# Eight-group cross network on one core: a joint first pass over two output tiles, tails copied by VectorE, and a rearranged last job

## Chip, cores and metric

The kernel runs on one core of one Trainium2 chip. The metric is the device time of one execution in microseconds (us), the median over several executions. A profile is one execution taken by the hardware profiler. Its span, from the first to the last recorded instruction, is about 1.8 us shorter than the device time of the same execution.

Engines are named as in the profile: PE is the matrix engine, PEld its weight load, ACT the scalar engine, DVE the vector engine, SP the engine that issues most DMAs ("SPq" and "ACTq" are rows of DMA issues).

## The reference

`x0` is [16384, 416], `ws` is [6, 416, 416], `bs` is [6, 416], all bf16.

```python
def reference(x0, ws, bs):
    x = x0
    for l in range(ws.shape[0]):
        proj = jnp.einsum('bd,de->be', x, ws[l]) + bs[l]
        x = x0 * proj + x
    return x
```

## The kernel before

The rows are cut into 8 groups of 2048. A job is one layer of one group. Data lie transposed on the chip, features on partitions: 416 features are three tiles of 128 and a "tail" of 32, and the 2048 rows are four chunks of 512 (`NJ = 4`). For one output tile, PE adds up the products with three input tiles (12 matmuls of 512 columns) and with the tails (4 matmuls on 32 partitions) in four PSUM banks; ACT evicts two banks at a time and adds the bias; DVE multiplies by x0 and adds x. Jobs of different groups alternate so that PE always has work. The program has eight banks and uses four per output tile, so an output tile has to wait for the eviction of the one before the last; where it comes too early the profile lists the wait (`PE ps L460 <- ACT tw L398`, 0.4 us in the changed kernel).

Group 0 starts from row-major loads that PE transposes. Group 1 is brought in by DMA transposes while group 0's first layer runs, and its tails are copied out of a staging tile (`Tb`) by four small DMAs:

```python
def load_group(g):
    ...
    turn(0)
    add("sp", lambda h: h.dma_start_transpose(Tb, x0[rows, D - P:D]), ...)
    turn(1)
    turn(2)
    for j in range(NJ):
        q = slice(j * T32, (j + 1) * T32)
        add("sp", lambda h, q=q, j=j: h.dma_start(x0s[s][q, XW:XW + CH], Tb[P - T32:P, j * CH:(j + 1) * CH]),
            reads=[("ost", 0, 0)], writes=[("x03q", s, j)], lane=f"x03_{s}", batch=g)
    if g == 1:
        load_wm(1, "sp")
        load_w3(1, "sp")
```

The last job (group 7, layer 5) is computed with rows on partitions, so that its result can be stored without a transpose. It goes in four quarters `kk`. For the residual x it needs x turned row-major: tiles 0 and 1 by DMA transposes (`rest_turn`), tile 2 and the tails by PE (`turn_last`, `turn_tails`). The store of group 6, whose result was turned just before, shares the DMA queue with them:

```python
def rest_turn(t):
    ...
    for j0, j1 in ((0, NJ),) if t == 0 else ((0, 2), (2, NJ)):
        if t and j0:
            store(LAST - 1, 0, 1)          # 416 KB of group 6
        add("sp", lambda h, j0=j0, j1=j1: h.dma_start_transpose(
            x5f[:, j0 * KK:j1 * KK, t * P:(t + 1) * P], xs[s][:, t * GC + j0 * CH:t * GC + j1 * CH]), ...)

def turn_tails(bks):                        # 16 small transposes, four banks
    for kk in range(KK):
        for j in range(NJ):
            r, q = quad(g, l, j)
            add("pe", lambda h, ...: h.matmul(
                psum_t(b)[:, kk * T32:(kk + 1) * T32], x3col(j, kk), ident[q, q], is_transpose=True, ...), ...)
    ...                                     # one ACT copy out of the four banks
# last job:
store(LAST - 1, 1, 2)
store(LAST - 1, 2, NJ)
...
for kk in range(1, KK):
    nat_rows(kk, bks[kk])
    for j in range(NJ):
        nat_full(kk, j, bks[kk][j], False)  # matmuls
        nat_out(kk, j, bks[kk])             # ACT
        ...                                 # DVE: nat_mul, nat_add
    if kk < last:
        nat_store(kk, 0, NJ)                # 416 KB each
```

## Time and profile before

| | kernel before |
|---|---|
| device time, median of 3 (lowest to highest) | 477.18 us (476.61 to 477.33) |
| span of the profiled execution | 476.1 us |
| PE, DVE, ACT busy | 98%, 85%, 72% |
| PE's waits at the second group's start | 0.8 us (input tile 2), 0.8 us (tails) |
| DVE's wait in the last job | 1.25 us (residual's second half-transpose) |

The lines behind this stand in the prediction. A row of the timeline reads: start in us, duration, engine and line of the program, operation, what it writes and reads, how many instructions, and in brackets how long the engine stood idle before it and what it then was waiting for. A row of the waits reads: what waited, for what, the sum in us, how often, the longest.

### The profile page before, as it was taken

The numbers are of one execution on the slowest core, as the hardware profiler recorded it, in microseconds if no ns is written. First come the engines' busy times: TensorE is split into PE (matmuls) and PEld (weight loads), VectorE is DVE, ScalarE is ACT, GpSimd is POOL, SyncE is SP. The second block draws the span as 40 slices with busy tenths as digits, with TensorE's granted clock in tenths as the row PEclk, the third lists the DMA queues.
The fourth block names the chain that finished last, engine by engine and source line by source line (L and its number), as shares of the span: only waits on it lengthen the run. The fifth ranks groups of instructions, "written<-read, shape, count | busy, mean of one in ns | idle before, by whom it ended". The sixth has DMA issues, their size and how long they took to land.

```text
span 476.1 us, 8364 instructions
## 1 busy us (share of the span) xinstructions
PE 467.7 (98%) x3356; PEld 193.4 (41%) x3356; DVE 403.3 (85%) x695; ACT 341.7 (72%) x371; POOL 5.8 (1%) x15
## 2 busy tenths in 40 slices
PE   8899999999999999999999999999999999999995
PEld 5344444444444444444444444444444444444342
DVE  2788888888888888898889879888888888888886
ACT  4577777777777777777777777777777777777785
POOL 1000000000000000000000000000000000000000
PEclk9999999999999999999999999999999999999999
DMA  8966860630102397369318941980000039025898
GB/s 223 161 163 150 174 122 1 144 79 0 30 7 43 64 224 154 81 143 246 77 25 195 220 95 26 175 264 0 2 12 23 8 64 240 12 45 122 226 192 247
DMA packets 138859, 53.31 MB, mean 112 GB/s; under 512 B 112442, under 2 KB 138308, under 8 KB 138820
## 3 DMA queue, kind: packets, MB, share of 16 engines
q1 hardware_dynamic: 138664, 52.67, 49.6%
q8 instruction: 26, 0.43, 0.4%
q10 hardware_dynamic: 156, 0.11, 0.1%
q14 instruction: 13, 0.11, 0.1%
HBM read 5.97 MB, written 13.63 MB: 41 GB/s over the span
## 4 chain that ended last, share of the span: by engine, by line
PE 90%; SPq 4%; DVE 3%; DMA 2%; ACT 0%; issue 0%; DVEq 0%
PE ps L457 75%; PE ps L478 7%; PE ps L498 7%; SPq L292 2%; DMA x<-x 1%; PE ps L472 1%; DVE x L887 1%; SPq L522 1%; DVE x L881 1%; DVE x L409 1%; DVE tw L404 1%; PE ps L489 1%; SPq L297 0%; ACT tw L395 0%; DMA x<-ost 0%; SPq L303 0%
## 5 line engine op out<-in xcount | busy, mean ns | idle before, releaser
L395 ACT ACTIVATE tw<-ps,bias 128x1024 bf16<-128x1024 f32 (+1 forms) x295 | 299.6, 1070 | 121.4 <-PE ps L478 82.2
L457 PE MATMUL ps<-x,wm 128*128 128x512 bf16 x1692 | 379.6, 380 | 1.3 <-DMA x<-in_x_dram 0.8
L457 PEld LDWEIGHTS ps<-x,wm 128*128 128x128 bf16 x1692 | 158.7, 98 | 215.3 <-issue 28.2
L404 DVE TENSOR_TENSOR tw<-tw,x 128x1024 bf16<-128x1024 bf16 (+1 forms) x285 | 192.8, 684 | 55.6 <-ACT tw L395 55.2
L409 DVE TENSOR_TENSOR x<-tw,x 128x1024 bf16<-128x1024 bf16 (+1 forms) x285 | 182.5, 681 | 0.0
L478 PE MATMUL ps<-x,w 32*128 32x512 bf16 x512 | 39.2, 379 | 0.8 <-DMA x<-ost 0.8
L498 PE MATMUL ps<-x,wm 128*32 128x512 bf16 x564 | 33.0, 380 | 0.0
L435 ACT ACTIVATE ts<-ps,bias 128x512 bf16<-128x512 f32 x47 | 28.7, 700 | 0.0
L498 PEld LDWEIGHTS ps<-x,wm 128*32 128x32 bf16 x564 | 13.8, 96 | 17.6 <-issue 5.3
L439 DVE TENSOR_TENSOR x<-ts,x 128x512 bf16<-128x512 bf16 x47 | 18.6, 418 | 2.4 <-DMA x<-x 2.4
L478 PEld LDWEIGHTS ps<-x,w 32*128 32x128 bf16 x512 | 7.8, 92 | 28.5 <-issue 27.1
L437 DVE TENSOR_TENSOR ts<-ts,x 128x512 bf16<-128x512 bf16 x47 | 18.6, 418 | 0.0
L821 PE MATMUL ps<-wm,x 128*128 128x416 bf16 x48 | 9.5, 340 | 0.0
L684 POOL COPY ost<-ot 128x512 bf16<-128x512 bf16 x6 | 4.3, 720 | 423.7 <-DMA ot<-x 423.7
L875 ACT ACTIVATE x<-ps 128x416 bf16<-128x416 f32 x16 | 7.7, 534 | 2.0 <-PE ps L821 1.9
L575 DVE COPY x<-ps 128x512 bf16<-128x512 bf16 x5 | 2.0, 422 | 8.2 <-PE ps L565 8.1
L577 ACT ACTIVATE x<-ps 128x512 bf16<-128x512 bf16 x7 | 3.8, 595 | 4.9 <-PE ps L565 4.9
L821 PEld LDWEIGHTS ps<-wm,x 128*128 128x128 bf16 x48 | 4.3, 98 | 4.2 <-issue 1.0
L887 DVE TENSOR_TENSOR x<-x,x 128x832 bf16<-128x832 bf16 (+1 forms) x9 | 4.8, 542 | 1.4 <-DMA x<-x 1.3
L489 PE MATMUL ps<-x,w 32*32 32x512 bf16 x188 | 5.9, 374 | 0.0
L472 PE MATMUL ps<-x,w 32*32 32x512 bf16 x208 | 5.6, 385 | 0.0
L881 DVE TENSOR_TENSOR x<-x,x 128x832 bf16<-128x832 bf16 (+1 forms) x10 | 4.8, 500 | 0.7 <-ACT x L875 0.7
(40 smaller groups left out, 32.0 us busy)
## 6 DMA issues: line engine op xcount, KB each, us to landing
out_dram<-ost SPq DMA_DIRECT2D x6, 1664.0 KB, 7.2
x<-x SPq DMA_DIRECT2D x24, 96.0 KB, 2.1
wm<-in_ws_dram SPq DMA_DIRECT2D x6, 312.0 KB, 3.4
x<-in_x_dram SPq DMA_DIRECT2D x8, 208.0 KB, 4.2
x<-in_x_dram SPq DMA_DIRECT2D x4, 416.0 KB, 8.0
x<-x SPq DMA_DIRECT2D x22, 64.0 KB, 2.0
out_dram<-x SPq DMA_DIRECT2D x3, 416.0 KB, 3.6
x<-ost SPq DMA_DIRECT2D x28, 32.0 KB, 2.0
```

The lines of the kernel that those rows point to most:

```text
L395: add("act", lambda h, a=a, w=w, b0=b0: h.activation(tw[r][:, a * CH:(a + w) * CH], psum[:, b0 * CH:(b0 + w) * CH], ACT_F.Identity, bias=b ...
L404: add("dve", lambda h, a=a, e=e: h.tensor_tensor(tw[r][:, a * CH:e * CH], tw[r][:, a * CH:e * CH], x0s[s0][:, i * GC + a * CH:i * GC + e * ...
L409: add("dve", lambda h, a=a, e=e: h.tensor_tensor(xs[so][:, i * GC + a * CH:i * GC + e * CH], tw[r][:, a * CH:e * CH], src(i, a, e), ALU.ad ...
L435: add("act", lambda h: h.activation(ts[r][:, :], bank(b), ACT_F.Identity, bias=bias[:, 3, l:l + 1], scale=1.0), reads=[("ps", b), "bias"], ...
L437: add("dve", lambda h: h.tensor_tensor(ts[r][:, :], ts[r][:, :], x03, ALU.mult), reads=[("ts", r)] + tok0, writes=[("ts", r)], release=True)
L439: add("dve", lambda h: h.tensor_tensor(x3s[so][:, :], ts[r][:, :], res, ALU.add), reads=[("ts", r)] + rtok, writes=[("x3", so), ("x3", so, ...
L457: add("pe", lambda h, t=t, j=j: h.matmul(bank(banks[j]), wm[l][:, t, ecols], src(t, j, j + 1), start=(first and t == 0), stop=(not first a ...
L472: add("pe", lambda h, q=q, j=j, r=r, c=c, o=o: h.matmul(psum[o, banks[j] * CH:(banks[j] + 1) * CH], w3[l][q, i * P + c * T32:i * P + (c + ...
L478: add("pe", lambda h, q=q, j=j, r=r: h.matmul(bank(banks[j]), w3[l][q, ecols], src[q, :], start=first, stop=not first, tile_position=(r * ...
L489: add("pe", lambda h, l=l, b=b, s3=s3, ri=ri, qi=qi, ro=ro, qo=qo: h.matmul(psum[qo, b * CH:(b + 1) * CH], w3[l][qi, NT * P:D], s3[qi, :], ...
L498: add("pe", lambda h, t=t, j=j, src=src, l=l, b=b, ro=ro, qo=qo: h.matmul(psum[qo, b * CH:(b + 1) * CH], wm[l][:, t, NT * P:D], src(t, j, ...
L821: add("pe", lambda h, t=t: h.matmul(bank(b, n=D), xcol(t, j, kk), wm[l][:, t, :], start=(first and t == 0), stop=(not first and t == NT - 1)),
```

## The change

The intent: at the start, let PE work on input tiles 0 and 1 of group 1 for two output tiles before it needs tile 2 and the tails, and take the tails' DMAs away. At the end, let the second half-transpose go directly behind the first, and use fewer and larger PE transposes for the tails so that fewer banks are held.

```diff
@@ load_group
-        for j in range(NJ):
-            ... h.dma_start(x0s[s][q, XW:XW + CH], Tb[P - T32:P, j * CH:(j + 1) * CH])
-        if g == 1:
-            load_wm(1, "sp")
-            load_w3(1, "sp")
+        if g > 1:
+            for j in range(NJ):
+                ... the same four DMAs
+            rotate_x03(g)
@@ before group 0's last tile
+    def second_tails():
+        for j in range(NJ):
+            add("dve", lambda h, q=q, j=j: h.tensor_copy(
+                x0s[s][q, XW:XW + CH], Tb[P - T32:P, j * CH:(j + 1) * CH]), ...)
+        load_wm(1, "sp") ... load_w3(2, "sp")
@@ rest_turn
-            if t and j0:
-                store(LAST - 1, 0, 1)
@@ the first two output tiles of group 1
+    def two_tiles(g, l):
+        bks = [job_banks(), job_banks()]
+        for t in (0, 1):
+            for i in (0, 1):
+                full(g, l, i, bks[i], True, False, ts_=[t])
+        full(g, l, 0, bks[0], True, False, ts_=[2])
+        rows32(g, l, 0, bks[0], False)
+        evacuate(g, l, 0, bks[0], list(range(NJ)), 2)
+        finish_tile(g, l)
+        rows32(g, l, 1, bks[1], False, inner=True)
+        full(g, l, 1, bks[1], False, False, ts_=[2])
+        evacuate(g, l, 1, bks[1], list(range(NJ)), 2)
+        finish_tile(g, l)
@@ turn_tails: four full transposes in one bank, two ACT copies
-            for j in range(NJ):
-                ... h.matmul(psum_t(b)[:, kk * T32:(kk + 1) * T32], x3col(j, kk), ident[q, q], is_transpose=True)
+            add("pe", lambda h, kk=kk: h.transpose(
+                psum_t(b)[:, kk * P:(kk + 1) * P], s3[:, kk * P:(kk + 1) * P], ident[:, :]), ...)
@@ last job
-    store(LAST - 1, 1, 2)
+    store(LAST - 1, 0, 2)
     store(LAST - 1, 2, NJ)
-    turn_tails([b0, b1, b2, b3])
+    turn_tails(b0)
```

More of the change, by code (lines that the diff above doesn't have):

```diff
@@ L300, in load_group, with rotate_x03 @@
         turn(2)
-        for j in range(NJ):
-            q = slice(j * T32, (j + 1) * T32)
-            add("sp", lambda h, q=q, j=j: h.dma_start(x0s[s][q, XW:XW + CH], Tb[P - T32:P, j * CH:(j + 1) * CH]),
-                reads=[("ost", 0, 0)], writes=[("x03q", s, j)], lane=f"x03_{s}", batch=g)
-        if g == 1:
-            load_wm(1, "sp")
-            load_w3(1, "sp")
+        if g > 1:
+            for j in range(NJ):
+                q = slice(j * T32, (j + 1) * T32)
+                add("sp", lambda h, q=q, j=j: h.dma_start(
+                    x0s[s][q, XW:XW + CH], Tb[P - T32:P, j * CH:(j + 1) * CH]),
+                    reads=[("ost", 0, 0)], writes=[("x03q", s, j)], lane=f"x03_{s}", batch=g)
+            rotate_x03(g)
+    def rotate_x03(g):
+        s = slot(g)
         if turn_of(g, 1):
@@ L448, in prefill, with full @@
             rotate(x3s[xtail[(g, l)]], x3s[so], n, [("x3", xtail[(g, l)])], ("x3", so), f"rot{so}", (g, l))
-    def full(g, l, i, banks, first, chunk_major, after_chunk=None, chunks=range(NJ)):
+    def full(g, l, i, banks, first, chunk_major, after_chunk=None, chunks=range(NJ), ts_=range(NT)):
         src, stok = x_src(g, l)
         ecols = slice(i * P, (i + 1) * P)
-        seq = [(t, j) for j in chunks for t in range(NT)] if chunk_major else \
-              [(t, j) for t in range(NT) for j in chunks]
+        seq = [(t, j) for j in chunks for t in ts_] if chunk_major else \
+              [(t, j) for t in ts_ for j in chunks]
         for t, j in seq:
@@ L462, in full, with rows32 @@
                 after_chunk(j)
-    def rows32(g, l, i, banks, first, small=False):
+    def rows32(g, l, i, banks, first, small=False, inner=False):
         src, stok = x3_src(g, l)
@@ L478, in rows32 @@
             add("pe", lambda h, q=q, j=j, r=r: h.matmul(
-                bank(banks[j]), w3[l][q, ecols], src[q, :], start=first, stop=not first,
+                bank(banks[j]), w3[l][q, ecols], src[q, :], start=first and not inner,
+                stop=not first and not inner,
                 tile_position=(r * T32, 0)),
@@ L536, in bass_standalone__cross_network_dcn__recsys_kernel @@
     load_group(1)
-    load_wm(2, "sp")
-    load_w3(2, "sp")
+    def second_tails():
+        s = slot(1)
+        for j in range(NJ):
+            q = slice(j * T32, (j + 1) * T32)
+            add("dve", lambda h, q=q, j=j: h.tensor_copy(
+                x0s[s][q, XW:XW + CH], Tb[P - T32:P, j * CH:(j + 1) * CH]),
+                reads=[("ost", 0, 0)], writes=[("x03q", s, j)])
+        load_wm(1, "sp")
+        load_w3(1, "sp")
+        rotate_x03(1)
+        load_wm(2, "sp")
+        load_w3(2, "sp")
     def keep_busy(n, b):
@@ L627, in first_job @@
         evacuate(g, l, 1, bb, list(range(NJ)), 2)
+        second_tails()
         full(g, l, 2, ba, False, True, lambda j: evacuate(g, l, 2, ba, [j], 1))
@@ L776, in bass_standalone__cross_network_dcn__recsys_kernel @@
     mode[len(items) - 1] = "RF"
+    def two_tiles(g, l):
+        assert items[:2] == [("tile", (g, l), 0), ("tile", (g, l), 1)]
+        bks = [job_banks(), job_banks()]
[10 more added lines that the diff above has]
+        finish_tile(g, l)
     first_job()
@@ L786, in bass_standalone__cross_network_dcn__recsys_kernel @@
             start_job(g, l)
+        if n == 0:
+            two_tiles(g, l)
+            continue
+        if n == 1:
+            continue
         if mode[n] in ("FR", "F1"):
@@ L844, in turned_out, with turn_tails @@
             add("dve", lambda h: h.tensor_copy(dst, sp_), **kw)
-    def turn_tails(bks):
+    def turn_tails(b):
         for kk in range(KK):
-            for j in range(NJ):
-                r, q = quad(g, l, j)
-                add("pe", lambda h, b=bks[j], j=j, kk=kk, q=q, r=r: h.matmul(
-                    psum_t(b)[:, kk * T32:(kk + 1) * T32], x3col(j, kk), ident[q, q], is_transpose=True,
-                    tile_position=(r * T32, 0)),
-                    reads=tok3 + ["ident"], writes=[("ps", bks[j])])
-        b = bks[0]
-        assert bks == list(range(b, b + NJ))
-        sp_ = psum[:, b * CH:(b + NJ) * CH].bitcast(BF16).rearrange("p (j c) -> p j c", j=NJ)[:, :, 0:KK * T32]
-        add("act", lambda h: h.activation(
-            x5n[:, :, :, NT * P:D], sp_.rearrange("p j (k f) -> p j k f", k=KK), ACT_F.Copy),
-            reads=[("ps", b) for b in bks] + ["x5 free"], writes=[("x5n", j, NT) for j in range(NJ)])
+            add("pe", lambda h, kk=kk: h.transpose(
+                psum_t(b)[:, kk * P:(kk + 1) * P], s3[:, kk * P:(kk + 1) * P], ident[:, :]),
+                reads=tok3 + ["ident"], writes=[("ps", b)])
+        sp_ = psum_t(b)[:, 0:KK * P].rearrange("p (k q f) -> p q k f", k=KK, q=NJ)
+        j = 0
+        while j < NJ:
+            r = quad(g, l, j)[0]
+            n = min(NJ - j, NJ - r)
+            add("act", lambda h, j=j, r=r, n=n: h.activation(
+                x5n[:, j:j + n, :, NT * P:D], sp_[:, r:r + n, :, :], ACT_F.Copy),
+                reads=[("ps", b), "x5 free"], writes=[("x5n", a, NT) for a in range(j, j + n)])
+            j += n
     def nat_rows(kk, bks, first=True):
```

## The prediction

> **What bounds the kernel now.** I read the page's busy shares first, then the waits of TensorE, then the chain that ended last, and then the timeline of the two ends of the kernel.
>
> ```profile
> PE 467.7 (98%) x3356; PEld 193.4 (41%) x3356; DVE 403.3 (85%) x695; ACT 341.7 (72%) x371; POOL 5.8 (1%) x15
> ...
> PE 90%; SPq 4%; DVE 3%; DMA 2%; ACT 0%; issue 0%; DVEq 0%
> ```
>
> TensorE (PE) is busy 98% of a span of 476.1 us, and 90% of the chain is PE. The middle has nothing to give: the diff leaves the number of large matmuls as it is. What can move is the 10% of the chain that is not PE, and PE's own waits:
>
> ```profile
> PE ps L457 <- DMA x<-in_x_dram: 0.8, 1, 0.8
> PE ps L478 <- DMA x<-ost: 0.8, 1, 0.8
> ...
> PE ps L832 <- ACT x L857: 0.4, 1, 0.4
> PE ps L850 <- ACT tw L395: 0.2, 1, 0.2
> ```
>
> The first two are each one wait at the start of the second group; the last two are in the final job. The timeline shows the first pair in place:
>
> ```profile
> 18.36 1.90 PE L457 MATMUL ps<-x,wm 128*128 128x512 bf16 x8
> ...
> 21.08 1.04 PE L457 MATMUL ps<-x,wm 128*128 128x512 bf16 x4 [0.82 <-DMA x<-in_x_dram]
> ...
> 22.89 0.61 PE L478 MATMUL ps<-x,w 32*128 32x512 bf16 x8 [0.77 <-DMA x<-ost]
> 23.32 2.12 ACT L395 ACTIVATE tw<-ps,bias 128x1024 bf16<-128x1024 f32 x2 [3.85 <-PE ps L478]
> 23.43 5.35 PE L457 MATMUL ps<-x,wm 128*128 128x512 bf16 x24
> ```
>
> Eight matmuls of the second group's first output tile use input tiles 0 and 1; then PE waits for input tile 2, which a DMA transpose is still bringing, and then for the tails (the last 32 features), which four small DMAs copy out of the staging tile. Those are issued at 19.04 to 20.96 and the last takes 1.88 us to land. From 23 us on PE waits for nothing until the last job. There the chain leaves PE:
>
> ```profile
> 452.40 0.38 PE ps L478 x4
> 452.79 2.11 ACT tw L395 x2
> ...
> 460.91 5.35 DMA x<-x
> ...
> 466.38 0.59 DVE x L887
> ```
>
> and the timeline of the DMA queue and of VectorE (DVE) shows why:
>
> ```profile
> 458.89 1.34 SPq L705 DMA_TRANSPOSE x<-x  x1
> 460.40 0.45 SPq L691 DMA_DIRECT2D out_dram<-ost  x1
> 460.91 1.44 SPq L705 DMA_TRANSPOSE x<-x  x1
> ```
>
> ```profile
> 464.54 0.59 DVE L887 TENSOR_TENSOR x<-x,x 128x832 bf16<-128x832 bf16 x1
> 466.38 0.59 DVE L887 TENSOR_TENSOR x<-x,x 128x832 bf16<-128x832 bf16 x1 [1.25 <-DMA x<-x]
> ```
>
> The second half-transpose of the last residual is issued behind a quarter store (416 KB), lands 5.35 us after issue, and DVE stands still for 1.25 us. From 466.38 DVE runs without a gap longer than 0.2 us to 473.8, so those 1.25 us reach the end.
>
> [...] the rate rises from about 205 GB/s to 355 at 461.5, when the store runs, and the three residual transposes take 3.2, 4.5 and 5.4 us to land, the longest being the one behind the store. [...] the 32 KB tail copies take 2.0 us (median)[...]. [...] The kernel before has no such copy on DVE; its 128x512 adds come every 0.33 us (two in 0.75), so I take 0.2 to 0.33 us for each 32x512 copy. [...]
>
> **The change, part by part.**
>
> One pass over input tiles. The first two output tiles of group 1 now run as 8 matmuls on input tile 0, 8 on tile 1, 4 on tile 2, 8 tail matmuls, 4 on tile 2. The pitch of a large matmul is 5.29/24 = 0.2204 us. Starting at 18.36, the first 16 end their issue at 18.36 + 3.53 = 21.89, after 21.08 when tile 2 was there: the 0.82 us wait goes. The tail matmuls come at 18.36 + 20 x 0.2204 = 22.77. Their data is now copied by DVE, in its queue behind the adds that end at 18.72: 4 copies, 0.8 to 1.3 us, done by 20.1. The 0.77 us wait goes as well. The 8 tail matmuls take 0.54 (the chain's step), the last 4 take 0.88: all of it is issued by 24.19. Before, the same work (12 of the 24 matmuls from 23.43) was issued by 23.43 + 12 x 0.2204 = 26.08. That is 1.89 us earlier: 1.59 of waits, and about 0.3 of drain around them.
>
> What is given back. The next job takes the banks of the first output tile. ScalarE (ACT) starts evicting them about 0.45 us after the tail matmuls start (22.89 to 23.32 before): at about 23.25. It needs 2.12 us for the two pairs of banks, so they come free at about 24.35 and 25.4. Before, PE had 12 matmuls between; now it has 4. It wants the first pair at 24.19 and waits 0.2, and after two matmuls (24.8) waits some 0.6 for the second: 0.8 to 0.9 back. Then 10 matmuls follow and the job's large matmuls end at about 25.45 + 2.2 = 27.7 against 28.7 before. **Gain at the start: 1.89 - 0.85 = 1.05 us.** From there PE is gapless, so it should reach the last job. The second eviction of ACT ends near 27.6, in time for the next banks. The weights of layer 1, needed at 24.2, are issued at 19.05 instead of 21.60 (the four tail DMAs ahead of them are gone); with 3.4 us to landing they are there at about 22.5.
>
> The copies on DVE cost 0.8 to 1.3 us of DVE in a stretch where its next result is needed some 4 us later (adds done at 21.4, the next job reads them from 24.2 on): no cost.
>
> No quarter store. The second half-transpose can be issued at 458.89 + 1.34 + 0.04 = 460.27, 0.64 earlier, with nothing between it and the first half. With the 3.2 us of an unhindered one it lands at about 463.5, with its old 5.35 at 465.6. Either way the 1.25 us wait (465.13 to 466.38) is cut to between 0 and 0.5.
>
> Four full transposes for the tails. 16 small ones need all four banks of the last tile evicted (PE waits 0.17), and then all four are held until one ACT copy of 0.60 us is done; the later transposes share a bank with them (0.35 of wait). Four 128x128 transposes, at about 0.07 us each (24 took 1.52), use one bank. Both waits go: PE reaches the second quarter of the job at about 462.8 instead of 463.12. The ACT copy becomes two of half the size, about 0.2 us more ACT time, off the path.
>
> What then ends last. A quarter of the last job costs PE 2.68 us (463.12, 465.80, 468.48), and DVE two multiplies and two adds of 0.51 to 0.61, about 2.25. DVE had been behind by its wait; without it PE paces again. Its last matmul ends at 471.2 - 0.35 = 470.9; the last eviction (0.53) ends at about 471.4, a multiply and two adds of 416 columns (0.33 each) follow: 472.4, against 473.82. **Gain at the end: up to 1.4; I take 1.25**, because the postponed 416 KB cost 1.25 us of the DMA's 335 GB/s near the end.
>
> Sum: 1.05 + 1.25 = 2.3 us; 477.18 - 2.3 = 474.9, or 0.5%.
>
> **Rivals.** First, bank waits give everything back at the start: if ACT began the first eviction later (after both tiles), PE would wait until 26 and gain nothing there: 475.9. Against it: the tail matmuls of the first output tile come before those of the second, and its eviction is queued first. Second, the store pushed behind the transposes makes DMA the bound at the end: 1664 KB of the sixth group and 1664 KB of the last have to leave after 463.3, which at 335 GB/s takes 9.9 us, to 473.2, before the last pieces, whose data is ready at 472.4 and which need about 1.8 us. That is close; if it binds, the end gains only 0.5: 475.6. Third, the late landing has nothing to do with the store: DMA moves almost nothing from 464.5 to 465.5 and the transpose lands only after that. If this pause sits behind the transpose wherever it goes, DVE waits about 0.4 and the end gains 0.9: 475.2. Fourth, upside: no bank wait at the start, which gives 474.0.
>
> **Range and chances.** Both gains are bounded by waits that are read off: at most 1.89 and about 1.4, so 473.9 is the best case; with one rival true it is 475.6 to 475.9, and runs spread by 0.7 us. I say 473.9 to 476.1. The 2% line is 467.6 and no wait in this trace is that large; slower by 2% would need a new stall of 9.5 us, for which nothing speaks.
>
> **What would show it.** Right: no wait of PE on a DMA between 18 and 24 us, instead two short waits of PE on the ACT eviction near 24 and 25, 0.8 us in sum; the first small matmuls of the next job about 1 us before 28.72; DVE copies of 0.2 to 0.33 us near 19; in the last job no DVE wait on the residual's transpose, and DVE waiting for ACT instead. Wrong: PE still waiting for input tile 2 (the weights' DMA in its way), a middle that loses the microsecond again, or final stores that land late.

The lower end of the 0.2 to 0.33 us for a copy, and of the 0.8 to 1.3 for four, rested on an assumption that no trace before the change shows. The upper end is the pitch of the 128x512 adds. Neither is in the sum. In the changed kernel the four copies take 0.28 to 0.29 us each and start every 0.30. A wait of PE for the eviction of banks that it reuses is measured there, too: 0.40 us at 25.55. The 0.3 us of "drain" are the difference 1.89 - 1.59. The 335 GB/s are the rate of the kernel before from 466 to 471 us (327 to 336 in each microsecond). The 0.2 us more for two ACT copies is an estimate without a source; two took 0.66 us together in the changed kernel, against 0.60 for the one before.

## The result, and the profile after

Six executions of the changed kernel have a median of 477.05 us (476.69 to 477.72); six of the kernel before in the same rounds 476.80 us (476.43 to 477.33). The ratio is 1.0005 with a 95% interval of 0.9992 to 1.0018. A ratio here is always the mean time of one kernel's fast runs over the mean of the other's of the same rounds, so it is not quite the ratio of the medians quoted. The 2.3 us that were predicted are not there, and 477.05 lies outside the range of 473.9 to 476.1.

The page of the changed kernel, busy shares and the chain that ended last, looks as if all had gone well:

```profile
PE 468.5 (99%) x3344; PEld 193.5 (41%) x3344; DVE 404.5 (85%) x699; ACT 342.1 (72%) x372; POOL 6.0 (1%) x15
...
PE 98%; ACT 1%; DVE 0%; issue 0%; DVEq 0%; POOL 0%; POOLq 0%
```

PE's part of the chain rose from 90% to 98%, and SP and DMA are no longer in it. That chain ends at the last instruction of an engine, and here it hides what matters. The start, in the timeline of the changed kernel:

```profile
18.52 4.49 PE L460 MATMUL ps<-x,wm 128*128 128x512 bf16 x20
18.89 1.19 DVE L547 COPY x<-ost 32x512 bf16<-32x512 bf16 x4
...
22.95 0.61 PE L481 MATMUL ps<-x,w 32*128 32x512 bf16 x8
...
25.55 2.33 PE L460 MATMUL ps<-x,wm 128*128 128x512 bf16 x10 [0.40 <-ACT tw L398]
...
27.82 0.43 PE L475 MATMUL ps<-x,w 32*32 32x512 bf16 x16
```

Twenty large matmuls go without a break, there is no wait on a DMA, the four copies take 1.19 us together, PE waits 0.40 us for a bank in one wait that the view shows, and the first small matmuls of the next job start at 27.82, against 28.72. The end, in the same view, with the DMA issues and the DVE adds of the residual:

```profile
458.00 2.72 SPq L720 DMA_TRANSPOSE x<-x  x2
...
460.89 1.13 SPq L708 DMA_DIRECT2D out_dram<-ost  x2
...
463.21 1.09 DVE L925 TENSOR_TENSOR x<-x,x 128x832 bf16<-128x832 bf16 x2
...
470.94 0.65 DVE L925 TENSOR_TENSOR x<-x,x 128x416 bf16<-128x416 bf16 x2
471.62 0.38 ACTq L932 DMA_DIRECT2D out_dram<-x  x1
```

The two residual adds follow each other at 463.21 with no wait between them, and DVE ends at 471.59; before it was 473.82. But the execution isn't over until the last store has landed, here at 474.59 us of a span of 475.1. The list of DMA issues (KB each, median us from issue to landing) has this for the very last store, before:

```profile
out_dram<-x ACTq DMA_DIRECT2D x1, 104.0 KB, 1.8
```

and after:

```profile
out_dram<-x ACTq DMA_DIRECT2D x1, 104.0 KB, 3.0
```

The same 104 KB land 1.2 us later than they did. So the gain of the last job was given back after all engines had finished.

**One clock for all kernels.** To say where time comes and goes I needed marks that don't shift with the arrival of the first weights. Three were taken from each trace: T1, the first 32x32 matmul of group 0's tails; T2, the first small 32x32 matmuls of the next job; T3, the start of the last group of such small matmuls, near 447 us. T3 - T2 is 418.93 or 418.94 us in all eleven traces that have both marks: the middle of the kernel neither gains nor loses. T1 itself lies anywhere from 17.2 to 18.1 us, with either kernel; PE's wait for the first weights is listed in six of the fourteen traces, with 0.3 to 1.4 us. That alone spreads the times by about a microsecond. So the start is judged by T2 - T1 and the end by what follows T3. All in us; "DVE end" is the end of DVE's closing DRAIN, 0.05 to 0.06 us after its last add. Each store leaves sixteen semaphore records in the trace, which I read as one for each of the 16 DMA engines; "15 engines" is the time of the fifteenth, "last landing" that of the sixteenth, and the difference of the two is called the lag below:

```
kernel (trace)              T2-T1   PE end  DVE end  15 engines  last landing
                                     ------ after T3, us -------------------
before (the page)           11.44    23.58   26.23     27.96       27.98
after (the page)            10.38    23.17   24.90     26.72       27.84
```

Against the first trace of the kernel before, the start gains 1.06, PE 0.41, DVE 1.33, and even 15 of 16 DMA engines gain 1.24; only the last engine gains 0.14. Two questions are open. Why is one DMA engine late? And why do the medians not even show the 1.06 us of the start?

### The profile page after: what moved, and what is told of

Same layout as the page of the kernel before. It is cut to its first block, busy times and chain, and to the rows that moved or that the text cites. A ratio compares the mean times of both kernels' runs of the same rounds, so it can differ in the third digit from the quotient of the medians.

```text
span 475.1 us, 8338 instructions
## 1 busy us (share of the span) xinstructions
PE 468.5 (99%) x3344; PEld 193.5 (41%) x3344; DVE 404.5 (85%) x699; ACT 342.1 (72%) x372; POOL 6.0 (1%) x15
## 4 chain that ended last, share of the span: by engine, by line
PE 98%; ACT 1%; DVE 0%; issue 0%; DVEq 0%; POOL 0%; POOLq 0%
PE ps L460 78%; PE ps L481 7%; PE ps L502 7%; PE ps L858 2%; PE ps L475 1%; PE ps L561 1%; PE ps L581 1%; PE ps L493 1%; ACT tw L398 0%; PE ps L869 0%; PE ps L902 0%; ACT x L913 0%; DVE x L919 0%; DVE x L925 0%; PE ps L907 0%; PE ps L601 0%
```

## The experiments

Twelve runs were made, in three rounds of four. Every one is given with the same marks.

```
kernel (trace)                  T2-T1   PE end  DVE end  15 engines  last landing
a1 before, again                10.02    23.55   26.23     27.96       27.97
a2 after, again                 10.38    23.17   24.90     26.63       27.92
a3 new start, old end           10.38    23.47   25.84     27.56       27.58
a4 old start, new end            9.83    23.17   24.90     26.64       28.32
b1 after, no group-6 store      10.38    23.17   24.89     26.62       26.64
b2 after, fetch moved           10.38    23.52   25.25     26.96       27.09
b3 before, fetch moved          10.03    24.72   26.44     28.15       28.16
b4 other order, fetch moved      9.83    23.52   25.24     26.97       27.14
c1 after, quarter store back    10.38    23.17   26.44     28.18       28.19
c2 after, fewer PE instr.           -    23.38   25.10     26.84       26.99
c3 before, fewer PE instr.          -    24.81   26.54     28.26       28.27
c4 other order, fewer instr.        -    23.54   25.27     27.00       27.11
```

(In c2 to c4 the small matmuls that mark T2 were replaced by others.)

### First round: repeat both kernels, then each half alone

**a1_before_again** is the kernel before, unchanged, profiled again.

> The kernel before, unchanged: a control for the noise, and a second trace of it. Its first trace was the slowest of its executions (477.9 us, the median of the others 476.8) and holds 1.5 us around 464 us in which packets on all 16 DMA engines stood still. Theory A (that pause was an accident of this one execution, so the waiting time at the end that I read off it is not in most executions): ratio 1.000 within 0.15%, and a trace whose span is about 475.0, without the pause, where the residual's second half-transpose lands under 4.5 us after issue. Theory B (the pause belongs to the kernel): the pause is there again at 464 us, span 475.5 to 476.1.

Measured: 477.07 us, ratio to before of the same rounds 0.9997 [0.9984, 1.0011], as it should be for the same kernel. The timeline of PE in this trace:

```profile
18.85 2.76 PE L457 MATMUL ps<-x,wm 128*128 128x512 bf16 x12
21.95 0.61 PE L478 MATMUL ps<-x,w 32*128 32x512 bf16 x8 [0.34 <-DMA x<-ost]
```

The twelve matmuls of the first output tile run through: input tile 2 is there in time. The wait for the tails is 0.34 us. In place of 1.59 us of waits there are 0.34, and T2 - T1 is 10.02 and not 11.44. The end repeats, as theory B had it: the second half-transpose lands 5.34 us after its issue again, behind the same kind of pause (17 long packets from 463.2 on), and DVE waits 1.29 us for it. The page of the first profile showed an unlucky start: its device time, 477.91 us, is above that of 34 of the 37 timed executions of this kernel in all rounds. Its first DMA transpose of group 1 kept SP for 3.68 us, against 2.1 to 2.6 in the other four traces of the old start.

**a2_after_again** is the changed kernel, unchanged, profiled again.

> The changed kernel, unchanged: ratio 1.000 within 0.15% to the kernel before, as in the result. Its last add on VectorE should again be near 471.6 us and the last bytes of the stores be acknowledged near 474.6, by one DMA engine that is 1.1 to 1.3 us behind the other 15 (theory C: the end is bound by the stores' queue, which is never empty from 462 on, and by one engine of it that lost a microsecond to an instruction fetch at 463.8). If the lag was an accident, all 16 engines end together near 473.5 and the span is about 474.

Measured: 477.29 us, ratio 1.0002 [0.9989, 1.0014]; T2 - T1 again 10.38, DVE end again 24.90, and one engine again late, by 1.29 us at the last store.

**a3_start_only** has the new start and the old end:

```diff
 # the changed kernel; the two bodies of turn_tails are left out
+            if t and j0:
+                store(LAST - 1, 0, 1)
-    def turn_tails(b):          # four full transposes
+    def turn_tails(bks):        # sixteen small ones
-    store(LAST - 1, 0, 2)
+    store(LAST - 1, 1, 2)
-    turn_tails(b0)
+    turn_tails([b0, b1, b2, b3])
```

> Only the new start: two output tiles in one pass and the tails copied by VectorE; the end as before, with the quarter store and 16 small transposes. In the trace of the changed kernel PE reached the first small matmuls of the next job 0.9 us before (27.82 against 28.72). Theory C (the gain at the start is real and lost at the end to the later stores): this kernel is 0.7 to 1.0 us faster than before, ratio 0.9979 to 0.9985. Theory D (the middle or the end swallows any gain of the start): ratio 0.9995 to 1.0005.

Measured: 477.06 us, ratio 0.9999 [0.9987, 1.0012]. Theory C had 0.9979 to 0.9985: it failed. T2 - T1 is 10.38. The new start costs the same in every trace, and the old one 9.83 to 10.03 in three traces of four: the new one loses 0.35 to 0.55 us against these. Its waits on banks are the reason. The waits of PE in the changed kernel name the larger:

```profile
PE ps L460 <- ACT tw L398: 0.4, 1, 0.4
```

The end is not quite the old one: the half-transpose landed 4.96 us after its issue, DVE waited 0.97 us for it, and the last landing is 0.39 us before that of a1.

**a4_end_only** has the old start and the new end (the same edit, in the other direction).

> Only the new end: no quarter store and four full transposes; the start as before. Theory C: the stores are postponed and end later, so this kernel is 0.5 to 1.2 us slower than before, ratio 1.001 to 1.0025, and adds up with the run of the start alone to the ratio of the whole change. Theory D (neither part does anything): ratio 0.9995 to 1.0005. My prediction on record would have it 1.25 us faster, ratio 0.9974.

Measured: 476.90 us, ratio 0.9997 [0.9985, 1.0010]. Theory C had it 0.5 to 1.2 us slower than before, which it is not. Here the old start waited only 0.15 us for the tails (T2 - T1 9.83). DVE ends 1.33 us earlier than in a1, as predicted; the last landing is 28.32, 0.35 us later than in a1. One DMA engine is 1.68 us behind the other fifteen.

Both halves alone are worth nothing in time: the start because the old waits are mostly short, the end because of the late engine.

### What the late engine was doing

The bandwidth view of the changed kernel, in slices of half a microsecond near the end (columns: slice, its length, busy time of each engine with the number of instructions, granted clock, mean busy share of the 16 DMA engines, in which overlapping packets count more than once, and GB/s):

```profile
core 0: us, PE busy (x) PEld busy (x) DVE busy (x) ACT busy (x) POOL busy (x), PEclk, DMA share, GB/s
...
472.50:473.00 0.50, 0.00 (x0) 0.00 (x0) 0.00 (x0) 0.00 (x0) 0.00 (x0) 1.00 0.75 245
473.00:473.50 0.50, 0.00 (x0) 0.00 (x0) 0.00 (x0) 0.00 (x0) 0.00 (x0) 1.00 0.07 22
473.50:474.00 0.50, 0.00 (x0) 0.00 (x0) 0.00 (x0) 0.00 (x0) 0.00 (x0) 0.70 0.07 20
```

From 473.0 on the mean share is 0.07, which is one engine of sixteen (0.06), and the rate is about a sixteenth of the 330 GB/s that ran before. The semaphore records, sixteen for each store, show where that engine lost its time (after):

```
store                       15 engines           the last one    behind by
first 832 KB of group 6     465.24 to 465.41        466.93          1.52
second 832 KB               467.80 to 468.11        469.51          1.40
quarter 0 of the last job   469.09 to 469.47        470.78          1.31
quarter 1                   470.34 to 470.85        472.06          1.21
quarter 2                   471.67 to 472.15        473.36          1.21
...
last 104 KB                 473.18 to 473.47        474.59          1.12
```

It lost 1.5 us before 467 and made up only 0.4 us in the rest: between 463 and 472 the rate does not fall below 270 GB/s in any microsecond, so the others are hardly ever idle, and the late one has no time to catch up in. The packet records show a suspect. Besides the two data queues there are two for instructions; this is one of them on the page of the kernel before (packets, MB, share of 16 engines):

```profile
q8 instruction: 26, 0.43, 0.4%
```

Its last packet in the changed kernel starts at 463.78, has 16,384 bytes and takes 0.96 us. It is one packet, so it is taken to occupy one engine; the records do not say which. I take the packets of this queue for fetches of PE's instructions, since they keep step with PE's work: the 26 of the changed kernel start between the 105th and the 3301st matmul, one for every 128 on average (100 to 160 from one to the next), which with as many weight loads are 256 PE instructions. PE does not wait for this one: in the changed kernel, as in the view of the kernel before below, it is busy 0.50 us in every 0.50 from 463.5 to 465.5. But, so the suspicion, it takes 1.5 us from one of the sixteen engines that the stores need.

In the kernel before the same fetch comes at 463.95, and there it falls near the end of the second half-transpose of the residual. The bandwidth view of before, around it:

```profile
core 0: us, PE busy (x) PEld busy (x) DVE busy (x) ACT busy (x) POOL busy (x), PEclk, DMA share, GB/s
463.50:464.00 0.50, 0.50 (x7) 0.26 (x4) 0.30 (x1) 0.50 (x3) 0.00 (x0) 1.00 1.26 236
464.00:464.50 0.50, 0.50 (x5) 0.27 (x4) 0.47 (x1) 0.50 (x1) 0.00 (x0) 1.00 4.36 105
464.50:465.00 0.50, 0.50 (x4) 0.27 (x3) 0.50 (x2) 0.50 (x2) 0.00 (x0) 1.00 0.02 2
465.00:465.50 0.50, 0.50 (x4) 0.29 (x3) 0.13 (x1) 0.50 (x2) 0.00 (x0) 1.00 0.08 9
```

The queue all but stands still for a microsecond, at 2 and 9 GB/s (this is what the expectations call all 16 engines standing still; the packet records name no engine): 21 packets of 832 bytes that began at 464.1 each last 1.51 to 1.59 us, where an ordinary one takes about 0.04 (the share of 4.36 in the second row is this: packets are counted where they begin). Their size tells whose they are: 832 bytes are one row of the output, so they belong to the store behind the transpose, while the transposes move 256 bytes in a packet. From 464.2 to 464.8 no packet starts at all; then 23 packets of 256 bytes, the rest of the transpose, start one after another from 464.9 to 465.5, and at 465.6 the stores go on. That, and not only the 416 KB of the quarter store, is why the transpose took 5.35 us. In the changed kernel the transposes have landed at 462.92, before the fetch.

So the theory for the end, at this point: one instruction fetch costs the kernel about 1.2 us wherever it falls in the last 12 us (too broad, as b3 and c3 will show). In the old order it stops the transpose and so DVE. In the new one the transpose escapes it, and it delays one DMA engine's part of the stores, which have no slack. The rivals were the prediction's own: the quarter store causes the long landing; or the postponed 416 KB make DMA as a whole the bound.

### Second round: take the load away, move the fetch

**b1_no_sixth_store** is the changed kernel without the two stores of group 6 in the last job. Its result is wrong (group 6 is not written).

```diff
-    store(LAST - 1, 0, 2)
-    store(LAST - 1, 2, NJ)
```

> The changed kernel without the two stores of the last group but one (1664 KB; the result is wrong on purpose, those rows stay unwritten). Theory C (the stores' queue sets the end, together with one DMA engine that an instruction fetch sets back): without them the queue runs empty before the last pieces, the last store lands 1.8 to 2.0 us after its issue instead of 3.0, the lag of the one engine is made up, and from the residual's last job on the kernel is 1.0 to 1.3 us shorter than the changed one; ratio to before 0.9970 to 0.9985. Theory F (the last stores take about 3 us to land anyway in the changed kernel, whatever is in the queue): ratio 0.9995 to 1.0005, landing still 3.0.

Measured: 475.71 us, ratio 0.9982 [0.9970, 0.9994]. The fetch still comes (462.66), at a time when the transposes have just landed (462.52) and no store has been issued yet (the first is at 464.17). The lag is gone (0.02 us) and the last store lands at 26.64. This is the gain that had been predicted for the end, 1.33 us against 27.97: with slack in the queue it is all there. It also shows that with the full load 15 engines are hardly later (26.63 to 26.72 against 26.62): DMA as a whole is not the bound, one engine is.

**b2_after_shifted_fetch** is the changed kernel with 128 instructions added to PE's queue, spread over the middle, that do nothing but add to an unused semaphore. If fetches follow PE's instructions, one for 256 on average as in the trace above, the last one moves forward by half a period.

```diff
+    pad = nc.alloc_semaphore("pad")
+    pe = pr.queue["pe"]
+    spaced = pe[:420]
+    for k in range(420, len(pe)):
+        if (k - 420) % 20 == 0 and k < 420 + 20 * 128:
+            spaced.append(Op("pe", lambda h: h.sem_inc(pad)))
+        spaced.append(pe[k])
+    pr.queue["pe"] = spaced
     pr.emit()
```

> The changed kernel, whole and correct, with 128 increments of a semaphore that nobody waits for on PE's sequencer, one to every 20 matmuls from the 420th on[...]. They do one thing: the last of PE's 16 KB instruction fetches, which came at the 3300th matmul (463.8 us, in the middle of the stores), comes 128 instructions, that is 64 matmuls, earlier, at about 455.5 to 456.5, where the DMA queue has a pause of half a microsecond. Theory G (that fetch sets one DMA engine back by 1.1 to 1.9 us, and this lag is what cancels the gain at the end): all 16 engines land the last store within 0.3 us of each other, at most 2.3 us after its issue, and the kernel is 0.9 to 1.3 us faster than before; ratio 0.9972 to 0.9982. If the lag stays, the fetch is not its cause: ratio 0.9995 to 1.0005. If the increments cost PE time, PE's stretch from the 800th to the 3200th matmul is longer than the 335.83 us of all runs so far.

Measured: 476.41 us, ratio 0.9998 [0.9985, 1.0011]. The last fetch moved from 463.8 to 452.8: it does belong to PE's instructions. The lag fell from 1.1 to 0.13 us, and the last landing from 27.84 to 27.09. So far the theory holds, but the ratio misses the 0.9972 to 0.9982 that was expected: by the marks the kernel is 0.36 us behind a1 at the start and 0.88 ahead at the end, 0.52 in all or 0.9989, and the interval holds both this and 1. The rest of the gain was spent elsewhere. Bandwidth in this kernel where the fetch now is:

```profile
453.00:453.50 0.50, 0.50 (x4) 0.21 (x3) 0.29 (x1) 0.50 (x2) 0.00 (x0) 1.00 3.08 196
453.50:454.00 0.50, 0.50 (x4) 0.27 (x3) 0.40 (x1) 0.50 (x1) 0.00 (x0) 1.00 0.94 14
454.00:454.50 0.50, 0.50 (x4) 0.21 (x3) 0.29 (x1) 0.29 (x2) 0.00 (x0) 1.00 0.08 10
```

The pause of the kernel before again, now in the transposes of group 6's result: the whole queue pauses for about 1.2 us. PE and DVE end 0.35 us later for it.

**b3_before_shifted_fetch** does the same to the kernel before.

> The kernel before with the same 128 increments on PE. In both of its traces the last instruction fetch fell into the second half-transpose of the residual, and all 16 engines then stood still for 1.5 us, which is the late landing that I put down to the quarter store. Theory G: with the fetch earlier this landing comes 3.2 to 4.0 us after issue in place of 5.3 (3.2 plus the 0.6 or so that the store takes), VectorE no longer waits for it, and the old kernel alone becomes 0.6 to 1.2 us faster than before; ratio 0.9975 to 0.9988. If the quarter store was the cause, as the prediction has it, the landing still takes about 5.3 us, and the ratio is 0.9995 to 1.0005.

Measured: 476.93 us, ratio 1.0017 [1.0001, 1.0032] (two of the six executions took 478.6 and 478.8). What this run was for is the second half-transpose, still behind its quarter store. It is issued at 459.99 and lands at 463.77, in 3.78 us, where it took 5.35; without the quarter store it takes 3.3 to 3.5 (3.54 in the changed kernel, 3.28 in a2 and a4). So the quarter store cost 0.2 to 0.5 us of landing and 0.6 of issue, and the fetch the rest. DVE's two residual adds now follow each other in this kernel too:

```profile
464.21 1.09 DVE L887 TENSOR_TENSOR x<-x,x 128x832 bf16<-128x832 bf16 x2
```

The time is no better, if anything worse, because the moved fetch (451.4, and one of another queue at 452.8) delayed the transposes of group 6 and with them ACT, which waits 1.23 us for one of them until 457.12, with its evictions queued behind; PE then waited for ACT in the last job:

```profile
PE ps L850 <- ACT tw L395: 0.9, 3, 0.4
```

PE ends 1.17 us later than in a1. One cost was exchanged for another.

This trace also corrects the theory. The longer program fetches once more, at 468.22, among the last job's stores. One engine is 0.76 us late in the store of quarter 1 and 0.01 us in the last one, since this queue has gaps to catch up in (15 GB/s between 470 and 471). So a fetch near the end does not cost time wherever it falls: the lag went from 0.76 to 0.01 us here, and only from 1.52 to 1.12 in the changed kernel, where the rate stays at 270 GB/s or more.

**b4_shifted_start_and_fetch** is b2 with another order at the start, in which the first output tile is finished before the second goes on. PE then has about 2.0 us of work (8 large matmuls at 0.22 us and 4 for the tails) before it needs the first banks again, and ACT took 2.12 us for the two pairs of a tile in the kernel before, half of it for the first, so by this estimate no bank wait is expected:

```diff
-        for t in (0, 1):
-            for i in (0, 1):
-                full(g, l, i, bks[i], True, False, ts_=[t])
-        full(g, l, 0, bks[0], True, False, ts_=[2])
+        full(g, l, 0, bks[0], True, False, ts_=[0])
+        full(g, l, 1, bks[1], True, False, ts_=[0])
+        full(g, l, 0, bks[0], True, False, ts_=[1, 2])
         rows32(g, l, 0, bks[0], False)
         ...
-        rows32(g, l, 1, bks[1], False, inner=True)
-        full(g, l, 1, bks[1], False, False, ts_=[2])
+        full(g, l, 1, bks[1], True, False, ts_=[1, 2])
+        rows32(g, l, 1, bks[1], False)
```

> The changed kernel with the same increments and another order at its start: the first tile's input tile 0, the second's input tile 0, then the first tile to its end with its tails and eviction, then the rest of the second. PE then has eight matmuls and four tail matmuls between the first tile's end and the next job, in place of four and four. Theory H (in the changed kernel the start costs two waits for evictions, 0.4 and 0.25 us, as much as the DMA waits it removes in most executions, 0.15 to 0.34): both waits go, the stretch from the 92nd to the 200th matmul takes 16.1 to 16.4 us in place of 16.82 (16.26 and 16.45 in the two newer traces of the old start), and the kernel is 0.3 to 0.6 us faster than the one with the increments alone; ratio to before 0.9960 to 0.9975.

Measured: 475.90 us, ratio 0.9984 [0.9972, 0.9996], with a right result; 0.9960 to 0.9975 was expected. T2 - T1 is 9.83, equal to the old start in a4, where that waited 0.15 us, and 0.55 us better than the change's own order; PE's timeline from 17.5 to 30 us lists no wait for a bank. The end is that of b2 (27.14). It is the best correct version that I found, 0.16% faster than the kernel before; small, but its interval does not reach 1.

### Third round: put the quarter store back, take the last fetch away

**c1_quarter_store_back** is the changed kernel with the quarter store between the two half-transposes again.

```diff
+            if t and j0:
+                store(LAST - 1, 0, 1)
-    store(LAST - 1, 0, 2)
+    store(LAST - 1, 1, 2)
```

> The changed kernel with the quarter store put back where it was, between the two half-transposes of the residual. Theory G (the late landing comes from PE's last instruction fetch falling into a transpose, and the quarter store only delays it by 0.6 us): the second half-transpose is then still moving when the fetch comes at 463 to 464, all 16 engines stand still and it lands 5.0 to 5.5 us after issue; or, if it is just ahead of the fetch, 3.6 to 4.0. In both cases no engine is left 1 us behind at the end, because the queue is 1.2 us shorter. Ratio to before 0.999 to 1.0005 with the pause, 0.997 to 0.9985 without.

Measured: 477.42 us, ratio 1.0011 [0.9991, 1.0030]. DVE waits again for the residual, and longer than in the kernel before. The half-transpose's issue and DVE's adds in the timeline:

```profile
460.01 1.48 SPq L722 DMA_TRANSPOSE x<-x  x1
...
463.22 0.58 DVE L927 TENSOR_TENSOR x<-x,x 128x832 bf16<-128x832 bf16 x1
465.70 0.59 DVE L927 TENSOR_TENSOR x<-x,x 128x832 bf16<-128x832 bf16 x1 [1.90 <-DMA x<-x]
```

The way is not the same as before, though. No stillness of all engines this time: fifteen of them have finished the transpose by 464.04, 4.0 us after its issue, and one, by this reading the one with the fetch of 463.55, at 465.58. So the fetch costs 1.5 us here too, but through one engine, because the transpose, and DVE's wait with it, ends only with the sixteenth record. And the lag that this engine carries on is 1.5 us in the first stores and 0.02 in the last one. The quarters come later now, the queue has gaps (the rate is 82 GB/s between 471 and 472), and in the gaps the late engine catches up. DVE ends at 26.44 and the last landing is 28.19. The quarter store had this much to do with it: it holds the transpose in the queue until the fetch arrives. The expectation named two cases, a pause of all engines with 5.0 to 5.5 us to landing, or 3.6 to 4.0 just ahead of the fetch; this was a third, with 5.57 us.

**c2_after_no_last_fetch**, **c3_before_no_last_fetch** and **c4_shifted_no_last_fetch** go the other way and take PE instructions away. Five output tiles in the middle use 4 matmuls of 128 columns of weights for their tails in place of 16 of 32, 60 matmuls fewer in all (3284 for 3344 in c2). c2 is otherwise the changed kernel, c3 the kernel before, c4 the kernel b4 without the added instructions.

```diff
-            rows32(g, l, i, banks, False, mode[n] == "F1")
+            f1_seen += mode[n] == "F1"
+            rows32(g, l, i, banks, False, mode[n] == "F1" and f1_seen > 5)
```

> The changed kernel with 60 fewer matmuls on PE (120 instructions): five of the tiles that run their tails as 16 small 32x32 matmuls run them as 4 of 32x128, as the other tiles do. PE's time should stay within 0.3 us. The last 16 KB fetch of PE instructions would come after the program's end, so it should not happen, and the one before it moves to about 449. Theory G: no packet over 300 ns from 455 us on, no lagging engine, last add to last landing 1.7 to 1.9 us; from the last batch of tails (447 us) to the end 27.1 to 27.3 us in place of 28.3 to 28.4; ratio to before 0.9970 to 0.9982, and 1.1 us faster than the changed kernel. If the lag of one engine stays without the fetch, theory G falls.

Measured: 476.69 us, ratio 0.9988 [0.9972, 1.0005], short of the 0.9970 to 0.9982 expected. The fetch of 463.8 is gone, as intended: the page counts 25 packets on the instruction queue instead of 26. But the one before it, at 445.1 in the changed kernel, moved to 453.2, into the same transposes of group 6 as in b2. The lag is 0.15 and the last landing 26.99, 0.85 us better than in the changed kernel, and DVE is 0.2 us later. The rearranged tiles cost about 0.5 us in the middle (T3 - T1 is 429.83 against 429.31), which takes most of it back.

> The kernel before with the same 60 matmuls fewer, so also without the last fetch, start and end otherwise as they were, quarter store included. Theory G: the residual's second half-transpose lands 3.6 to 4.0 us after issue in place of 5.3; VectorE does not wait for it; last batch of tails to the end 27.3 to 27.8 us in place of 28.46; ratio 0.9978 to 0.9990. If the quarter store were the cause: landing 5.3 us, 28.4 us, ratio 0.9995 to 1.0005. Its start gives one more sample of the old waits: 9.8 to 10.1 us from the first tails to the first small matmuls, against 11.44 in the first trace.

Measured: 477.00 us, ratio 1.0006 [0.9987, 1.0025]. A miss as an experiment on "no fetch": the longer program of the kernel before still fetches twice, at 453.1 and 469.9 (26 packets). As in b3, the late fetch puts one engine 0.96 us behind in one store and 0.01 in the last. The second half-transpose behind its quarter store lands 3.80 us after issue, as in b3, and PE and DVE end late for the same reason as there.

> The version that should beat both: the changed kernel without the last fetch and with the start in the other order (first tile to its end, then the second). Start 9.8 us (as in the run with the shifted start), end 27.1 to 27.3 us: 1.2 to 1.3 us less at the end than before and 0.1 to 0.2 less at the start than a usual execution of before; ratio 0.9965 to 0.9978.

Measured: 476.44 us, ratio 0.9986 [0.9969, 1.0003]. As b4: landing 27.11, lag 0.11. The better order at the start is worth as much with or without added instructions, but this interval reaches 1, and 0.9965 to 0.9978 was expected.

### How often it happens

The pauses are not confined to the end. In the packet records of the kernel before there are six places where at least eight data packets take over 0.8 us together; five of them start 0.1 to 1.0 us after the start of an instruction fetch. In the changed kernel it is six of six. In the middle of the kernel they show no cost to PE: in these two traces T3 - T2 is 418.93 or 418.94 us, as in the other nine that have both marks. Not every fetch does this: in a4 one starts at 461.65, half a microsecond before the last transpose has landed, and the transpose does not stand still; the fetch itself then takes 1.83 us in place of 0.96, and the lag in the first store after it is the largest of all, 2.28 us.

## Why the prediction was wrong, point by point

**The start: the removed waits.** The prediction took 1.59 us of waits from one trace and subtracted them. They were removed; there is no wait on a DMA in any trace of the new start. But in other traces of the old start these waits are 0.34 (a1), 0.35 (b3), 0.68 (c3) and 0.15 (a4). The term "1.59 of waits" is the one that failed: against the first trace the gain is 11.44 - 10.38 = 1.06, just what was predicted, and against a1 it is 10.02 - 10.38, a loss of 0.36.

**The start: what is given back.** The bank waits of 0.8 to 0.9 us were predicted in the right place, after the first and second pair of banks, and nearly in the right size. The view lists one wait of 0.40, but it measures from modelled ends. By the starts of the single matmuls in the changed kernel, which else come 0.22 apart, PE starts one at 24.55, 0.40 after the one before, and one at 25.55, 0.78 after: 0.18 and 0.56 lost, 0.74 in sum, for the 0.2 and 0.6 foreseen. Against b4's order T2 - T1 is 0.55 longer (10.38 against 9.83). This part repeats in every execution, while the waits that it was traded for come and go. The first rival's outcome, no gain at the start, is what the typical executions show; its reason is not, since the bank waits are no larger than predicted and the waits removed are smaller.

**The copies on DVE.** Four in 1.19 us, predicted 0.8 to 1.3, and nobody waits for them: right.

**The end: DVE and PE.** Predicted: no wait on the half-transpose, PE 0.35 earlier, the last add up to 1.4 earlier. Measured: no wait on the transpose, 0.41 and 1.33, and DVE waits for ACT instead (0.41 us at 462.70), as foreseen. This is right. The reason given for the old landing was only half right. The quarter store costs 0.2 to 0.5 us of landing by itself (3.78 against 3.3 to 3.5); the fetch adds about 1.5 (5.35 against 3.78).

**The end: from the last add to the last landing.** The step that failed is "the last pieces, whose data is ready at 472.4 and which need about 1.8 us". The last of them needed 474.59 - 471.59 = 3.00 us from the end of the last add. For fifteen engines the step holds (473.47, 1.88 us); the sixteenth was 1.12 us late. The second rival had the right place: late stores, and a gain of 0.5 at most; measured is 0.13 against a1. Its reason, DMA as a whole at its limit, holds for one engine of sixteen. Its sum is slightly off, too: it takes a KB as 1000 bytes, but the page's 416 KB are 512 rows of 832 bytes, so 3328 KB at 335 GB/s need 10.2 us and not 9.9, to 473.5. That is where the fifteen engines ended, so the full queue and the last data came to a draw, and b1 shows that emptying the queue gains the fifteen no more than 0.1 us. The third rival had the right suspicion, a pause that doesn't belong to the store. But the pause does not follow the transpose: it comes with the fetch, which moves when PE's instruction count is changed (from 463.8 to 452.8 with 128 instructions more, b2).

**The sum.** Predicted -1.05 - 1.25 = -2.3 us. From the marks, the changed kernel against a1: +0.36 at the start and -0.13 at the end, +0.23 us. The medians say 477.05 - 476.80 = +0.25.

**What stays open.** Why a fetch on one engine can stop what is queued on the others is not shown; that they coincide, and that the pause moves with the fetch, is. That the late engine is the one that carried the fetch is inferred, since the packet records name no engine. Whether a fetch met in a transpose stops nearly everything (before, a1, a3) or only delays one engine (c1), or spares the transpose and delays the stores (a4), can't be told beforehand from these traces. How the waits of the old start are spread over executions is known from five traces only. And no correct kernel was found that has the 26.6 of b1: each place to which the fetch was moved cost 0.2 to 0.35 us in the transposes of group 6.

## What to carry to other kernels

A wait that is read from one execution is a sample: the DMA waits at the start were 1.59 us in one trace and 0.15 to 0.68 in four others. Profile the same kernel twice before subtracting such a wait, and don't trade it for a bank wait that comes every time (0.55 us here, b4 against the change). When a gain is to be had in the last microseconds, follow the last store to its landing on every DMA engine: here the chain of engine instructions was 98% PE while one DMA engine in sixteen was 1.12 us late (1.29 in a2, 1.68 in a4). Count the instruction fetches among the DMA traffic: 128 instructions more on PE moved the last one from 463.8 to 452.8 (b2), away from the stores, and cut the lag from 1.12 to 0.13 us.
